# Linear attention and two expert layers: the first chunk's weights decoded over four slots of attention

## The chip, the cores and the metric

The kernel runs on one core of a Trainium2 chip. The metric is the time of the program on the device, in microseconds, as the median of several runs. Three runs of the kernel before gave 1057.95, 1059.56 and 1063.15 us.

## The reference, cut to what matters

```
phi(x) = [exp(p), exp(-p)],  p = x @ w_phi - max|x @ w_phi|      # per row, 2 x 128 features
kv = phi(k).T @ v;  z = sum over rows of phi(k)                   # per batch and head
attn = (phi(q) @ kv) / (phi(q) @ z + 1e-6)                        # (4, 8, 576, 64)
x = attn as 2304 tokens x 512
x = (sigmoid(x @ w_gate) * (x @ w_val)) @ w_out                   # d_ff 1536
out = leaky(x @ w_in2) @ w_out2                                   # d_ff 2048, slope 0.01
```

Attention's inputs are float32; the five weight matrices of the two layers are float64. The kernel reads those as pairs of int32 and builds from each a high and a low part in fp32r, and every product of a layer is three matmuls: high by high, high by low, low by high.

## The kernel before, in words

Attention is worked in 16 head pairs, (b, c) with b the batch and c the pair of heads; one pair is worked in one **slot** of the loop at line 516. A slot's order is written out by hand as a string of pieces in `ORDERS`, and `SLOTS` says which string each of the 17 slots takes (lines 502 to 511). Pieces of the slot's own pair n are: `tk`, `tq`, `tr` transpose k, q and the remaining 64 rows on TensorE (`ps_t`); `pk`, `pq` project them (`ps_p`) and take the maximum away on VectorE (L337, L339); ScalarE makes the features of k (`ka`, L346); `kv` multiplies them with v (L385, L386); `qr`, `qf` transpose the projected q (`ps_r`, `ps_q`, L397, L403) and ScalarE takes their exps (L406). Of the pair before, o, the slot computes numerator and denominator (`nn`, `ps_n`, L435), and sends the denominators on a round trip: `nm1` moves them to 9 per partition (`d`, L444), `nm2` takes reciprocals on VectorE (L449), writes them to DRAM (`rd`, L451), reads them back spread over the partitions (`rb`, L454), and GpSimd multiplies (L457). Of the pair before that, oo, `nm3` splits the normalised output into a high part on ScalarE (`xh`, L48) and a low part on VectorE (`xl`, L49).

Two streams are laid into the slots. A piece `d` takes a step of `first_weights`, which fetches the raw words of chunk 0's three matrices (512 KB each half, L116) and decodes them in six halves, each by six instructions on VectorE (L96, L99, L101, L103, L105, L108) and two on ScalarE (L97, L106); it has 22 steps. A piece `M` takes a unit of `moe_units`: three matmuls of chunk 0's gated products (`pg`, `pv`, 128x512) for batch b, or of the product with w_out (`po`). A unit of kk needs the normalised output of pair kk of its batch, and is left out while that isn't there (`ready`). 78 units exist; what the slots don't take is worked behind the loop, and then chunk 0 of the last batch, the other chunks and the second layer follow.

The strings are not the order in which instructions stand in the engines' queues. The program is recorded in the strings' order, and a scheduler then orders each engine's queue by what it expects to be ready; it pulls units of the gated product ahead as fillers. Each engine works its queue in that order. What the strings, the barrier at line 518 and buffers allow is what the change can move. In the names below, xh_78 and xl_79 are the halves for pairs 0 and 1 of batch 0, xh_80 and xl_81 those for pairs 2 and 3.

Of the kernel before, what the change touches and what calls it, by code (L numbers as in the profile page):

```python
# [19 lines left out]
def linear_attention_moe(ctx, tc, q, k, v, w_phi, w_gate, w_val, w_out, w_in2, w_out2, out):  # L20
# [5 lines left out]
    KD = DM // 128  # L26
# [210 lines left out]
    ld = att.enter_context(tc.tile_pool(name="ld", bufs=2))  # L237
# [41 lines left out]
    def load_pair(b, c):  # L279
        for nm, src in (("k", k), ("q", q)):  # L280
            t = ld.tile([128, J, 2, D], F32, tag=nm, name=nm)
            for h in range(2):
                nc.sync.dma_start(out=t[:, :, h], in_=src[b, 2 * c + h, 0:MAIN, :].rearrange("(p j) d -> p j d", j=J))
            nat[nm, b, c] = t
            if (nm, b, c) == ("k", 0, 0):
                for h in range(2):
                    nc.sync.dma_start(out=wbd[64 * h:64 * h + 64, h * NF:(h + 1) * NF], in_=w_phi)
        if c % 2 == 0:
            for nm, src in (("k", k), ("q", q)):
                t = ld.tile([128, 2, D], F32, tag=nm + "r", name=nm + "r", bufs=1)  # L290
                for h in range(2):
                    nc.sync.dma_start(
                        out=t[64 * h:64 * h + 64],
                        in_=src[b, 2 * c:2 * c + 4, MAIN:S, :].rearrange("(i h) s d -> h s i d", h=2)[h],
                    )
                nat[nm + "r", b, c // 2] = t
        vf = nat["v", b, c] = vfs[c % 2]
        for h in range(2):
            vs = v[b, 2 * c + h]
            nc.sync.dma_start(out=vf[:, 0:J, 65 * h:65 * h + 64], in_=vs[0:MAIN].rearrange("(p j) d -> p j d", j=J))  # L300
            nc.sync.dma_start(out=vf[64 * h:64 * h + 64, J, 66 * h:66 * h + 64], in_=vs[MAIN:S])
# [121 lines left out]
    def num(p, h):  # L423
        uh = wk.tile([128, S], F32, tag=f"u{h}", name=f"u{h}", bufs=2)
        for n in range(2):
            if n:
                yield
            cs = slice(288 * n, 288 * n + 288)
            ps2 = ps_a.tile([128, 288], F32, tag=f"kv{n}", name="ps_n")
            for s in range(2):  # L430
                i = 2 * h + s
                w = [z[:, s, 65 * h:65 * h + 128] for z in p.kvz]
                x = [f[:, cs] for f in p.qf[i]]
                if len(w) == 1:
                    nc.tensor.matmul(ps2, w[0], x[0], start=s == 0, stop=s == 1)  # L435
                else:
                    mm3(ps2, *w, *x, s == 0, s == 1)
            nc.scalar.copy(uh[:, cs], ps2)
        p.u.append(uh)

    def norm1(p):
        p.d = wk.tile([128, 9], F32, tag="d", name="d", bufs=2)
        for h in range(2):
            nc.sync.dma_start(out=p.d[64 * h:64 * h + 64], in_=p.u[h][64 - h:65 - h, :])  # L444

    def norm2(p):
        r = wk.tile([128, 9], F32, tag="r", name="r", bufs=2)
        nc.vector.tensor_scalar_add(p.d, p.d, 1e-6)
        nc.vector.reciprocal(r, p.d)  # L449
        rd = dr.tile([2, S], F32, tag="rd", name="rd", bufs=4)  # L450
        nc.sync.dma_start(out=rd.rearrange("h (p e) -> (h p) e", e=9), in_=r)  # L451
        p.rb = wk.tile([128, S], F32, tag="rb", name="rb", bufs=3)
        for h in range(2):
            nc.sync.dma_start(out=p.rb[64 * h:64 * h + 64], in_=rd[h:h + 1, :].to_broadcast([64, S]))  # L454
        for h in range(2):
            sl = slice(64 * h, 64 * h + 64)
            nc.gpsimd.tensor_tensor(out=p.rb[sl], in0=p.u[h][sl], in1=p.rb[sl], op=ALU.mult)  # L457

    def norm3(p):
        b, c = p.b, p.c  # L460
        split(p.rb[:, 0:MAIN], xpart(xh, b, c), xpart(xl, b, c))
        rs = slice(REM * b, REM * b + REM)
        split(p.rb[:, MAIN:S], xh[B][:, c, rs], xl[B][:, c, rs])

    def new_pair(b, c):
        p = Pair()
        p.b, p.c = b, c
        p.kf, p.tq, p.qf, p.u = [], [], [], []
        return p
# [11 lines left out]
    def moe():  # L481
        if m_next[0] is None or ready[0] < m_next[0]:
            return
        m_next[0] = next(m_gen, None)

    def moe_units():
        for b in range(B - 1):
            h = {}
            for kk in up1(0, b, h):
                yield KD * b + kk + 1  # L490
            for _ in down1(0, b, h):
                yield 0

    def step(gen, k=1):
        for _ in range(k):
            next(gen, None)
# [4 lines left out]

    ORDERS = [
# [7 lines left out]
    ]  # L510
    SLOTS = [0, 1, 2, 1, 5, 4, 3, 6, 3, 4, 3, 4, 3, 6, 5, 6, 3]
    m_gen = moe_units()
    m_next = [10 ** 6]
    dec = first_weights()
    split(wbd, wbh, wbl)
    for i in range(NP + 1):
        oo, o, n = o, n, (new_pair(*pairs[i]) if i < NP else None)
        if i == KD:
            step(dec, 100)
            p0.close()  # L520
            pools["hp"] = mid.enter_context(tc.tile_pool(name="hp0", bufs=2))
            pools["tp"] = mid.enter_context(tc.tile_pool(name="tp0", bufs=3))
            pools["po"] = ps_m
            m_next[0] = next(m_gen)
        ln = iter(())
        for piece in ORDERS[SLOTS[i]].split():
            if piece == "M":
                moe()
            elif piece == "d":
                if 1 <= i < KD:  # L530
                    step(dec)
            elif piece == "ld":
                if i + 1 < NP:
                    load_pair(*pairs[i + 1])
            elif piece[:2] == "nn":
                if o:
                    if piece[2:] in ("0", "2"):
                        ln = num(o, int(piece[2]) // 2)
                    next(ln, None)
            elif piece == "nm1":  # L540
                if o:
                    norm1(o)
            elif piece == "nm2":
                if o:
                    norm2(o)
            elif piece == "nm3":
                if oo:
                    norm3(oo)
                    ready[0] += 1
            elif n:  # L550
                fn, *arg = {
                    "tk": (t_k,), "tq": (t_q,), "tr": (t_r,), "pk0": (p_k, 0), "pk1": (p_k, 1), "pkr": (p_kr,),
                    "pq0": (p_q, 0), "pq1": (p_q, 1), "pqr": (p_qr,), "qr": (q_r,), "qf0": (q_f, 0), "qf1": (q_f, 1),
                    "kv0": (kv_main, 0), "kv1": (kv_main, 1),
                }[piece]
                fn(n, *arg)
# [339 lines left out]
```

## Time and profile before

| | |
|---|---|
| median of three runs | 1059.56 us |
| profiled execution | 1060.74 us, its span 1059.0 us |
| granted clock of TensorE, mean | 0.998 |
| TensorE busy | 1038.1 us (98%) |
| VectorE busy | 739.7 us (70%) |
| ScalarE busy | 455.8 us (43%) |
| GpSimd busy | 50.5 us (5%) |

In the rows PE is TensorE, PEld its weight loads, DVE VectorE, ACT ScalarE, POOL GpSimd and SP the engine that issues the transfers. Matmuls overlap, so the length of one is more than the distance to the next. Behind an arrow in brackets stands the idle time ahead of an instruction and what ended it. Attention runs from the start to about 270 us; slot 1 begins with its first `ps_n` at 22.0 us, slot 2 at 37, slot 3 at 57.7, slot 4 at 71.1, slot 5 at 86.7.

### The profile page before, as it was taken

To read this page: it belongs to the slowest core of one execution; us is meant where nothing else is said; L and a number is where in the kernel's file an instruction comes from. 1 tells how busy PE (TensorE), PEld (TensorE's weight loads), DVE (VectorE), ACT (ScalarE), POOL (GpSimd) and SP (SyncE) were. 2 spreads that over 40 slices of the span, in tenths; PEclk is the share of its full clock that TensorE was granted. 3 is DMA by queue.
4 is the path that set the end of the run, shared out by engine and by line. 5 is a ranking of instruction groups with operands and counts; after the bars stand their busy time and mean duration, and the time that the engine had idled before them with its cause. 6 is when DMAs were issued, how large, how long until landed. Compare 5 with 4: busy or idle time off the path is not lost.

```text
span 1059.0 us, 14600 instructions
## 1 busy us (share of the span) xinstructions
PE 1038.1 (98%) x5506; PEld 885.6 (84%) x5506; DVE 739.7 (70%) x1309; ACT 455.8 (43%) x954; POOL 50.5 (5%) x49
## 2 busy tenths in 40 slices
PE   7999999999999999999999999999999999999998
PEld 6788988889788888888888888888888888888886
DVE  4964877766469976385383457995797887979555
ACT  4666676767445332132131134475343333433221
POOL 0112121212200000000000000000000000000000
PEclk9999999999999999999999999999999999999999
DMA  5532233232174322021020013254162542515143
GB/s 144 149 86 71 68 101 78 70 85 55 52 270 119 102 71 68 1 80 40 1 80 1 1 41 150 95 193 143 56 229 76 173 148 91 178 61 179 47 161 131
DMA packets 96006, 104.46 MB, mean 99 GB/s; under 512 B 66112, under 2 KB 66240, under 8 KB 95936
## 3 DMA queue, kind: packets, MB, share of 16 engines
q1 hardware_dynamic: 95936, 103.52, 31.4%
q8 instruction: 44, 0.72, 0.3%
q14 instruction: 26, 0.21, 0.1%
HBM read 87.10 MB, written 16.33 MB: 98 GB/s over the span
## 4 chain that ended last, share of the span: by engine, by line
PE 87%; DVE 4%; DMA 4%; SPq 2%; ACT 2%; issue 1%; POOL 1%; POOLq 0%; ACTq 0%; DVEq 0%
PE ps_u L54 13%; PE ps_u L53 13%; PE ps_u L52 13%; PE ps_p L52 11%; PE ps_p L54 11%; PE ps_p L53 11%; PE kv L385 4%; PE ps_n L435 2%; DMA rb<-rd 1%; DVE ql L420 1%; DMA raw<-in_moe_w_gate_dram 1%; PE ps_q L403 1%; PE ps_t L318 1%; PE kv L386 1%; POOL rb L457 1%
## 5 line engine op out<-in xcount | busy, mean ns | idle before, releaser
L53 PE MATMUL ps_u<-xl,w 128*128 128x512 f32 (+1 forms) x592 | 213.5, 361 | 0.2 <-DVE xl L49 0.2
L52 PE MATMUL ps_u<-xh,w 128*128 128x512 f32 (+1 forms) x592 | 213.3, 361 | 0.0
L54 PE MATMUL ps_u<-xh,w 128*128 128x512 f32 (+1 forms) x592 | 212.8, 361 | 0.1
L52 PEld LDWEIGHTS ps_u<-xh,w 128*128 128x128 f32 x592 | 111.8, 189 | 17.7 <-ACT w L106 0.3
L54 PEld LDWEIGHTS ps_u<-xh,w 128*128 128x128 f32 x592 | 111.7, 189 | 17.6 <-DVE w L108 0.5
L53 PEld LDWEIGHTS ps_u<-xl,w 128*128 128x128 f32 x592 | 111.8, 189 | 17.5 <-DVE xl L49 0.5
L48 ACT CAST gh<-q 128x512 fp32r<-128x512 f32 (+1 forms) x134 | 76.2, 576 | 91.6 <-DVE q L664 89.9
L810 DVE TENSOR_TENSOR acc<-acc,ps_p 128x512 f32<-128x512 f32 x126 | 86.3, 685 | 39.7 <-PE ps_p L54 39.0
L52 PE MATMUL ps_p<-w,gh 128*128 128x512 f32 x288 | 112.1, 390 | 0.0
L53 PE MATMUL ps_p<-w,gh 128*128 128x512 f32 x288 | 112.0, 389 | 0.0
L54 PE MATMUL ps_p<-w,gl 128*128 128x512 f32 x288 | 111.7, 389 | 0.0
L49 DVE TENSOR_TENSOR gl<-q,gh 128x512 fp32r<-128x512 f32 (+1 forms) x134 | 83.9, 632 | 32.3 <-ACT gh L48 31.6
L664 DVE SCALAR_TENSOR_TENSOR q<-q,ps_u 128x512 f32<-128x512 f32 (+1 forms) x54 | 33.8, 626 | 90.0 <-PE ps_u L54 81.8
L640 DVE TENSOR_TENSOR acc<-acc,ps_p 128x512 f32<-128x512 f32 (+1 forms) x100 | 62.3, 632 | 24.6 <-PE ps_p L54 23.7
L53 PE MATMUL ps_p<-gl,w 128*128 128x512 f32 (+1 forms) x216 | 79.0, 366 | 0.0
L675 ACT ACTIVATE q<-q 128x512 f32<-128x512 f32 x48 | 30.2, 632 | 113.3 <-DVE q L753 113.2
L54 PE MATMUL ps_p<-gh,w 128*128 128x512 f32 (+1 forms) x216 | 78.8, 365 | 0.0
L52 PE MATMUL ps_p<-gh,w 128*128 128x512 f32 (+1 forms) x216 | 78.2, 366 | 0.0
L753 DVE TENSOR_TENSOR q<-ps_u,q 128x512 f32<-128x512 f32 x80 | 54.9, 688 | 24.9 <-PE ps_u L54 19.3
L106 ACT CAST w<-m 128x512 fp32r<-128x512 f32 x68 | 41.4, 619 | 68.2 <-DVE m L105 43.0
L97 ACT ACTIVATE e<-e,ebias 128x512 int32<-128x512 int32 x68 | 48.7, 722 | 43.5 <-DVE e L96 43.0
L662 ACT ACTIVATE q<-ps_u 128x512 f32<-128x512 f32 (+1 forms) x54 | 29.5, 549 | 86.9 <-PE ps_u L54 81.8
(142 smaller groups left out, 2051.5 us busy)
## 6 DMA issues: line engine op xcount, KB each, us to landing
w<-td SPq DMA_DIRECT2D x56, 512.0 KB, 4.7
raw<-in_moe_w_out_dram SPq DMA_DIRECT2D x28, 512.0 KB, 3.7
raw<-in_moe_w_in_dram SPq DMA_DIRECT2D x16, 512.0 KB, 3.7
td<-w SPq DMA_DIRECT2D x16, 512.0 KB, 2.7
raw<-in_moe_w_gate_dram SPq DMA_DIRECT2D x12, 512.0 KB, 4.1
raw<-in_moe_w_val_dram SPq DMA_DIRECT2D x12, 512.0 KB, 4.0
rb<-rd SPq DMA_DIRECT2D x32, 144.0 KB, 3.2
k<-in_k_dram SPq DMA_DIRECT2D x32, 128.0 KB, 2.9
```

The costliest lines, as they stand in the source:

```text
L48: nc.scalar.copy(hi, src)
L49: nc.vector.tensor_tensor(out=lo, in0=src, in1=hi.bitcast(F32), op=ALU.subtract)
L52: nc.tensor.matmul(ps, lh, rh, start=first, stop=False, **kw)
L53: nc.tensor.matmul(ps, lh, rl, start=False, stop=False, **kw)
L54: nc.tensor.matmul(ps, ll, rh, start=False, stop=last, **kw)
L97: nc.scalar.activation(out=e, in_=e, func=ACTF.Relu, scale=8.0, bias=ebias)
L106: nc.scalar.copy(hi, mf)
L385: nc.tensor.matmul(ps[:, h], p.kf[j // 2][:, j % 2, h, s, :], vf[:, j, 64 * h:64 * h + 65], start=(h, j) == (0, 0), stop=False)
L640: nc.vector.tensor_tensor(out=a, in0=a, in1=po, op=ALU.add)
L664: nc.vector.scalar_tensor_tensor(out=th, in0=th, scalar=1.0, in1=ps[1], op0=ALU.add, op1=ALU.mult)
L753: nc.vector.tensor_tensor(out=o, in0=x, in1=y, op=ALU.add)
L810: nc.vector.tensor_tensor(out=a, in0=a, in1=po, op=ALU.add)
```

## The change

The strings for slots 1 and 2 have 6 pieces `d` each in place of 15. Slot 4 takes the string of slot 2, with six `d` and no `M`, in place of one with five `M`. The end of decoding and the start of the units move from slot 4 to slot 5 (`KD` is 4).

```diff
-        "nn0 d tk tq d nn1 tr pk0 d d d pk1 nm3 nn2 d nn3 d pqr pq0 nm1 d pq1 d pkr d kv0 nm2 ld qr d d kv1 d qf0 qf1 d d",
...
+        "nn0 tk tq nn1 tr pk0 d pk1 nm3 nn2 d nn3 pqr pq0 nm1 d pq1 pkr d kv0 nm2 ld qr d kv1 qf0 qf1 d",
...
-    SLOTS = [0, 1, 2, 1, 5, 4, 3, 6, 3, 4, 3, 4, 3, 6, 5, 6, 3]
+    SLOTS = [0, 1, 2, 1, 2, 4, 3, 6, 3, 4, 3, 4, 3, 6, 5, 6, 3]
...
-        if i == KD:
+        if i == KD + 1:
             step(dec, 100)
...
             elif piece == "d":
-                if 1 <= i < KD:
+                if 1 <= i <= KD:
                     step(dec)
```

VectorE, the middle of slot 2, before. L96 to L108 are decoding, L337 and L339 the projections' maximum and its subtraction (`t` for k, `tr` and `tqr` for the remaining rows).

```order
L96 TENSOR_SCALAR e<-raw 128x512
L99 TENSOR_SCALAR m<-raw 128x512
L337 TENSOR_REDUCE m<-ps_p 128x4
L108 TENSOR_TENSOR w<-m,w 128x512
L101 SCALAR_TENSOR_TENSOR m<-raw,m 128x512
L103 SCALAR_TENSOR_TENSOR e<-raw,e 128x512
L339 TENSOR_TENSOR t<-ps_p,m 128x512
L105 SCALAR_TENSOR_TENSOR m<-m,e 128x512
L337 TENSOR_REDUCE m<-ps_p 128x4
L96 TENSOR_SCALAR e<-raw 128x512
L339 TENSOR_TENSOR t<-ps_p,m 128x512
L108 TENSOR_TENSOR w<-m,w 128x512
```

The same place now:

```order
L108 TENSOR_TENSOR w<-m,w 128x512
L99 TENSOR_SCALAR m<-raw 128x512
L101 SCALAR_TENSOR_TENSOR m<-raw,m 128x512
L337 TENSOR_REDUCE m<-ps_p 128x4 x2
L339 TENSOR_TENSOR t<-ps_p,m 128x512 x2
L103 SCALAR_TENSOR_TENSOR e<-raw,e 128x512 x2
L337 TENSOR_REDUCE m<-ps_p 128x2 x2
L339 TENSOR_TENSOR tr<-ps_p,m 128x256
L339 TENSOR_TENSOR tqr<-ps_p,m 128x256
L105 SCALAR_TENSOR_TENSOR m<-m,e 128x512
L49 TENSOR_TENSOR xl_79<-rb,xh_78 128x512
```

Where eight decoding instructions stood around the maxima of k before, three stand ahead of them and three behind, and the low part of pair 0's output has moved up to here.

ScalarE in slot 4, from the casts of the transposed inputs (`xhi`, `xrhi`) to the cast of pair 2's output (`xh_80`), before:

```order
L48 CAST xhi<-ps_t 128x512
L438 COPY u_897<-ps_n 128x288
L48 CAST xhi<-ps_t 128x512
L48 CAST xrhi<-ps_t 128x128 x2
L438 COPY u_897<-ps_n 128x288
L346 ACTIVATE kar<-tr 128x2x128 x2
L438 COPY u_948<-ps_n 128x288
L346 ACTIVATE ka<-t 128x4x128 x4
L438 COPY u_948<-ps_n 128x288
L48 CAST xh_80<-rb 128x512
L48 CAST xh_94<-rb 128x64
```

The same place now, with one cast of decoding (L106) in it:

```order
L48 CAST xhi<-ps_t 128x512
L438 COPY u_855<-ps_n 128x288 x2
L106 CAST w<-m 128x512
L48 CAST xrhi<-ps_t 128x128
L438 COPY u_910<-ps_n 128x288
L48 CAST xh_80<-rb 128x512
L346 ACTIVATE ka<-t 128x4x128 x4
L48 CAST xrhi<-ps_t 128x128
L438 COPY u_910<-ps_n 128x288
L48 CAST xhi<-ps_t 128x512
L346 ACTIVATE kar<-tr 128x2x128 x2
L48 CAST xh_94<-rb 128x64
```

The cast of xh_80 stood behind the four exps of `ka` and both casts of transposed inputs; it now stands ahead of the exps and of the second cast.

TensorE in slot 4, from the projection of the remaining rows to the first product with xh_80, before:

```order
L52 MATMUL ps_p<-wbh,xrhi 128x256
L53 MATMUL ps_p<-wbl,xrhi 128x256
L54 MATMUL ps_p<-wbh,xrlo 128x256
L385 MATMUL kv<-vf_124,ka 128x65 x8
L386 MATMUL kv<-vf_124,kar 128x130
L385 MATMUL kv<-vf_124,ka 128x65 x2
L52 MATMUL pg<-xh_80,w 128x512
L385 MATMUL kv<-vf_124,ka 128x65 x4
L53 MATMUL pg<-xl_81,w 128x512
L54 MATMUL pg<-xh_80,w 128x512
```

The place of that product now:

```order
L53 MATMUL ps_p<-wbl,xhi 128x256
L54 MATMUL ps_p<-wbh,xlo 128x256
L324 MATMUL ps_t<-ident,kr 128x128
L435 MATMUL ps_n<-qf,kvzf_134 128x288 x3
L54 MATMUL pv<-xh_78,w 128x512
L324 MATMUL ps_t<-ident,qr 128x128
L52 MATMUL pg<-xh_80,w 128x512
L318 MATMUL ps_t<-ident,q 128x128 x4
L52 MATMUL ps_p<-wbh,xrhi 128x256
L53 MATMUL ps_p<-wbl,xrhi 128x256
L54 MATMUL ps_p<-wbh,xrlo 128x256
L385 MATMUL kv<-vf_124,ka 128x65 x4
```

The product with xh_80 stood within the kv products; it now stands ahead of the transposes of q, of the remaining rows' projection and of all kv products.

## Rows read from the trace of the kernel before

**Rows 1.** The page: busy time of each engine, its share of the span, and instructions.

```profile
PE 1038.1 (98%) x5506; PEld 885.6 (84%) x5506; DVE 739.7 (70%) x1309; ACT 455.8 (43%) x954; POOL 50.5 (5%) x49
```

**Rows 2.** Table by stretch: stretch, length, busy us of each engine (instructions), clock, DMA, GB/s.

```profile
22.00:36.60 14.60, 14.50 (x93) 12.71 (x93) 13.09 (x25) 9.46 (x24) 0.00 (x0) 0.88 0.58 142
36.60:57.70 21.10, 17.21 (x94) 13.04 (x94) 20.04 (x38) 14.18 (x36) 2.90 (x2) 1.00 0.48 125
57.70:71.10 13.40, 13.39 (x96) 11.95 (x95) 7.72 (x14) 8.34 (x23) 2.83 (x2) 1.00 0.26 63
71.10:86.70 15.60, 15.56 (x110) 13.69 (x109) 9.43 (x20) 9.61 (x27) 2.85 (x2) 1.00 0.37 89
86.70:284.00 197.30, 191.00 (x1337) 172.08 (x1338) 136.54 (x248) 130.51 (x359) 37.00 (x24) 1.00 0.29 72
284.00:1059.00 775.00, 770.72 (x3684) 647.98 (x3682) 544.53 (x948) 275.51 (x473) 2.84 (x2) 1.00 0.31 103
```

**Rows 3.** Chain of waits, 40 to 58 us: its shares by line.

```profile
by line: DMA raw<-in_moe_w_out_dram 23.8%; DVE m L337 17.0%; DVE w L108 14.4%; DVE e L96 7.7%; DVE m L101 6.7%; DVE t L339 6.7%; DVE e L103 6.7%; DVE m L105 6.7%; PE ps_q L403 4.9%; DVE tq L339 4.2%; DVE m L99 3.7%; issue 3.0%; PE ps_n L435
```

**Rows 4.** Waits of TensorE, 15 to 90 us: total, times, longest (us).

```profile
PE ps_n L435 <- ACT qf L406: 3.2, 2, 2.6
PE ps_q L403 <- DVE tq L339: 1.6, 1, 1.6
```

**Rows 5.** VectorE by line, 22.0 to 86.7 us: busy us, mean ns, idle time before.

```profile
L105 DVE SCALAR_TENSOR_TENSOR m<-m,e 128x512 f32<-128x512 f32 x6 | 4.1, 684 | 0.0
L99 DVE TENSOR_SCALAR m<-raw 128x512 int32<-128x512 int32 x5 | 2.1, 419 | 0.0
```

**Rows 6.** Timeline of all engines, 69 to 83 us: start, length (us), instruction.

```profile
71.70 0.57 SPq L451 DMA_DIRECT2D rd<-r  x1
74.23 1.22 SPq L454 DMA_DIRECT2D rb<-rd  x2
77.73 2.92 POOL L457 TENSOR_TENSOR rb<-u,rb 64x576 f32<-64x576 f32 x2 [11.48 <-DMA rb<-rd]
80.97 0.76 ACT L48 CAST xh<-rb 128x512 fp32r<-128x512 f32 x2
```

**Rows 7.** Timeline of TensorE, the same stretch.

```profile
70.06 0.82 PE L403 MATMUL ps_q<-ident,tq 128*128 128x128 f32 x6
70.64 0.48 PE L52 MATMUL pg<-xh,w 128*128 128x512 f32 x1
71.13 0.75 PE L435 MATMUL ps_n<-qf,kvzf 128*128 128x288 f32 x2
...
79.95 0.28 PE L52 MATMUL ps_p<-wbh,xrhi 128*128 128x256 f32 x1
80.07 0.28 PE L53 MATMUL ps_p<-wbl,xrhi 128*128 128x256 f32 x1
80.31 1.90 PE L385 MATMUL kv<-vf,ka 128*128 128x65 f32 x16
```

**Rows 8.** Timeline of all engines, 138 to 147 us (slot 7).

```profile
142.07 0.40 PE L52 MATMUL po<-gh,w 128*128 128x512 f32 x1
142.30 0.40 PE L53 MATMUL po<-gl,w 128*128 128x512 f32 x1
142.32 0.77 ACT L48 CAST xh<-rb 128x512 fp32r<-128x512 f32 x2 [2.09 <-POOL rb L457]
144.41 0.36 PE L52 MATMUL ps_p<-wbh,xhi 128*128 128x256 f32 x1 [1.24 <-DVE xl L49]
```

**Rows 9.** Line 451, the transfer rd<-r, up to 140 us: issue to landing.

```profile
DMA to landing us min/median/max: 1.4/2.1/4.4
```

**Rows 10.** Table by stretch, around two gaps of TensorE.

```profile
19.40:22.10 2.70, 0.08 (x2) 0.04 (x1) 1.11 (x4) 1.36 (x3) 0.00 (x0) 1.00 1.11 276
22.10:25.50 3.40, 3.40 (x10) 2.58 (x11) 2.82 (x6) 2.45 (x8) 0.00 (x0) 0.53 0.38 79
...
53.00:57.30 4.30, 2.65 (x18) 2.15 (x18) 4.28 (x10) 1.58 (x7) 0.00 (x0) 1.00 0.31 69
```

2 rows, old and new, of the table ORDERS are left out of this document.

## The prediction

> **What bounds the kernel now.** I read the page's busy shares first: TensorE is busy for 1038.1 of 1059.0 us, so a change can pay only where TensorE stands still, 21 us in all [rows 1]. The table by stretch, cut at the points where a slot's first product of the numerator starts on TensorE, says where that is [rows 2]. Slot 1 (22.0 to 36.6) loses 0.10 us, slot 2 (36.6 to 57.7) loses 21.10 - 17.21 = 3.89, slots 3 and 4 lose 0.01 and 0.04, the other attention slots and the end of chunk 0 together 197.30 - 191.00 = 6.30, and the 775 us behind them 4.28. The part of slots 1 to 4 is thus 4.04 us, nearly all of it in slot 2. VectorE explains it: in slot 2 it is busy for 20.04 of 21.10 us, in slots 3 and 4 for 7.72 of 13.40 and 9.43 of 15.60. The chain of waits through slot 2 agrees; by lines it is VectorE's decoding, its reductions and the transfers of raw weights, with little of TensorE [rows 3]. The waits of TensorE name what came late: slot 2's q projections for 1.6 us, and once 2.6 us for the first features (of 3.2), in the gap ahead of slot 1 [rows 4].
>
> So decoding is not spread over three slots now. The order on VectorE has 12 of its 36 instructions beside slot 1's work and 24 beside slot 2's; none are left for slot 3. After the change I count 11, 12, 7 and 6 over slots 1 to 4.
>
> **The change part by part.** Slot 2 loses 12 decoding instructions on VectorE. Of the six kinds, two take about 0.42 us like L99 and four about 0.68 like L105 [rows 5], 0.60 on the mean: 12 x 0.60 = 7.2 us, which leaves 20.0 - 7.2 = 12.8 us beside 17.2 us of TensorE. Slot 1 shows what such a slot loses: VectorE is 13.09 of 14.60 there, fuller than slot 2 will be, and TensorE loses 0.10 [rows 2]. Bounds: all 3.89 us saved, or, if the 1.6 us for q stays, 2.3. I take 3.5, nearer the upper end since slot 1 is the nearest row.
>
> Slot 3 gains 7 instructions, 4.2 us: VectorE 7.7 + 4.2 = 11.9 of 13.4, as full as slot 1. One residual cast of a decoded weight (L108) stands between the two of the transposed inputs, which puts the q part of the projection back by 0.6 us. Bounds 0 and 1.2 (the wait of 1.24 us in rows 8, where a projection came late); I take +0.4. Slot 4 gains 6 instructions, 3.6 us: 13.0 of about 16, which alone costs nothing.
>
> The gated products do not begin later in the built order, though their code does: products that are ready are pulled up as fillers. TensorE has 11 of them by the end of slot 4 before and 18 now, and 55 and 61 left behind the last slot's transposes. Each keeps TensorE for 0.23 us (start to start in rows 8) wherever it stands, so the sum is unchanged and I cost this at 0. The cover is that TensorE is full at the end of chunk 0.
>
> What costs is where one of them now stands in slot 4. Gated product kk = 2 needs the normalised output of pair 2 (xh_80), and it now stands ahead of the transposes of q in TensorE's queue; ScalarE's cast that makes xh_80 stands ahead of the four exps of ka. Before, cast and product stood behind them. Both queues now stop until POOL has done pair 2. When is that? Before, slot 3's last product of kv with the values is followed by slot 3's last transposes at 70.06; then the value loads on SP come free, rd is issued at 71.70 behind them, rb at 74.23, POOL runs from 77.73 to 80.65 and the cast starts at 80.97 [rows 6]. Limited by POOL alone, xh_80 is there at 80.65 + 0.6 = 81.25, that is 11.2 us behind the last kv product. SP's order keeps the loads ahead of rd, so I keep the 11.2. From the last kv product to slot 4's start TensorE now has eight transposes (six start in 0.58 us, rows 7, so 0.8) and four gated products (0.9), so xh_80 comes 11.2 - 1.7 = 9.5 us into slot 4. TensorE gets to the product sooner: the work from 71.13 to 80.31 [rows 7] is 9.2 us, and of it the q projection (12 products, 0.12 from start to start), the remainder's (6), four transposes (0.4) and two gated products (0.46) are not ahead of it any more, three gated products (0.7) are: 9.2 - 1.4 - 0.7 - 0.4 - 0.5 + 0.7 = 6.9 us. TensorE waits for 9.5 - 6.9 = 2.6 us. Behind it stand the transposes of q and the kv products, behind the cast the ka exps (2.2 us) and the cast of q; the two sets of 16 kv products, 1.9 us each in rows 7, cover most of those. The nearest row is in slot 7 of the kernel before, where the same cast came before the exps: ScalarE stood for 2.09 us and TensorE for 1.24 [rows 8]. Bounds: rd took 2.1 us to land on the median, 1.4 at least and 4.4 at most [rows 9], so 2.6 - 0.7 = 1.9 and 2.6 + 2.3 = 4.9. I take 2.5.
>
> A gap of 2.7 us ahead of slot 1 was followed by 3.4 us at a granted clock of 0.53, the lower of the two levels (1.2 of 2.4 GHz), while the 1.65 us that TensorE lost between 53.0 and 57.3 changed nothing: 1.00 there and behind it [rows 2, 10]. The Trainium skill (TensorE: Matmul & The Clock Gate, Part 1) says that idling puts TensorE back to 1.2 GHz until it has been active again; both rows can be read that way, and by it the change may pay for its new gap twice. That rule is the second rival's. The gap stands between the two cases; in the sum I leave the clock at 1.00.
>
> The other slots keep their number of gated products in the code, but the built order puts 6 in place of 15 into slot 6 and moves others. They lose 6.30 us now; I take 0, and 2 either way as the bound: 9 fillers of 0.23 us are 2.1.
>
> Sum: -3.5 + 0.4 + 2.5 = -0.6 us. The profiled execution took 1060.74 us, so 1060.1; it lies 1.2 above the median of the three runs, 1059.56, by which it is 1059.0. I say 1059.2.
>
> **The rivals.** First, the gain is kept: pair 2's chain comes in time, because slot 2 runs faster and its loads are out sooner, and slot 4 does not wait. For it: SP's order has one load fewer between rd and rb. Against it: the 11.2 us hang on slot 3's own end, not on slot 2. Then -3.5, up to -3.9 with slot 3 free of cost: 1059.56 - 3.6 = 1056.0.
>
> Second, slower: pair 2's hold in slot 4 is 4.9 us, for which rd at its slowest is enough, and the clock falls behind it. At 0.53 for 3.4 us the loss is 3.4 x 0.47 = 1.6. Sum -3.5 + 0.4 + 4.9 + 1.6 = +3.4, so 1063.0. It decides from a hold of 3.1 us, where the gain is gone. For it: the two queues that stop, and the row of the low clock. Against it: slot 7's 1.24.
>
> Third, the change moves no decoding that matters: the q path of slot 2, not decoding, sets its length, and slot 2 saves only 2.3 us while slot 4 holds for 2.5 and slot 3 costs 0.4: +0.6, 1060.2. The full VectorE of slot 2 speaks against it.
>
> **How the numbers follow.** The forecast has 0.50, with 1057.0 to 1061.5 of its own from the bounds of the hold and the later slots; the first rival 0.24, the second 0.20, the third 0.06. Low: the first rival with 1 us from the later slots, 1055.0. High: the second with 0.8 from the later slots, 1063.8. About 0.5%, 5.3 us, is what a measurement of this kernel can tell from no change. Faster than 1054.3 needs the first rival and 2 us from the later slots: 0.05 and 0.01 for the rest. Slower than 1064.9 needs the second near its upper bound, 0.07, and 0.02 for the rest. That leaves 0.85 for no difference.
>
> **What would show it.** Right: slot 2 about 17.5 us long with under 0.8 us of TensorE's idle time; a wait of 1.5 to 4 us at a gated product pg for ScalarE's cast of xh in slot 4, and ScalarE idle there for POOL; slot 3 with under 1 us. The first rival shows no wait of TensorE over 1 us between 36 and 86 us. The second shows a granted clock near 0.5 behind slot 4's gap. I am wrong altogether if the time moves by over 5 us, which these four slots cannot give or take: then the later slots or the weights' decoding behind attention have moved.

## The result, and the profile after

The changed kernel takes 1069.80 us (median of 7 runs, 1064.89 to 1072.68) and the kernel before 1059.52 beside it: ratio 1.0089, 95% interval 1.0066 to 1.0112. Forecast were 1059.2, between 1055.0 and 1063.8, with 0.09 for slower: the forecast was wrong. The profiled execution took 1069.80 us, its span 1068.0, which is 9.0 more than before.

First the page's busy times after, which answer to [rows 1], then the table by stretch, cut as in [rows 2] where each slot's numerator starts (columns as there); the last cut is where slot 15's transposes end.

```profile
PE 1043.7 (98%) x5506; PEld 889.4 (83%) x5506; DVE 740.6 (69%) x1309; ACT 456.1 (43%) x954; POOL 51.9 (5%) x49
```

```profile
22.00:36.80 14.80, 14.50 (x93) 12.84 (x93) 12.52 (x25) 8.99 (x23) 0.00 (x0) 0.88 0.58 145
36.80:53.10 16.30, 16.11 (x97) 13.42 (x97) 14.20 (x28) 11.61 (x31) 3.46 (x2) 1.00 0.56 151
53.10:66.90 13.80, 13.79 (x98) 12.26 (x98) 11.62 (x22) 9.93 (x26) 3.18 (x2) 1.00 0.36 82
66.90:89.50 22.60, 19.84 (x111) 17.23 (x111) 12.08 (x24) 10.38 (x29) 2.80 (x2) 0.85 0.26 63
89.50:274.60 185.10, 177.15 (x1253) 158.28 (x1254) 128.22 (x235) 122.20 (x334) 34.29 (x22) 1.00 0.29 73
274.60:1068.00 793.40, 786.44 (x3763) 661.03 (x3761) 553.64 (x961) 284.72 (x498) 6.08 (x4) 1.00 0.30 101
```

TensorE is busy for 5.6 us longer with the same 5506 matmuls and idle for 3.4 longer. Busy time that grows at an equal count can come from the clock, and the rows show one new stretch for it: slot 4 is 7.0 us longer than in [rows 2], at a mean clock of 0.85. Slot 2 is 4.8 us shorter and slot 3 0.4 longer. The last two rows answer to these two of the kernel before, cut at the same points of its program:

```profile
86.70:267.90 181.20, 176.39 (x1265) 160.36 (x1265) 127.21 (x235) 122.18 (x335) 33.76 (x22) 1.00 0.30 76
267.90:1059.00 791.10, 785.33 (x3757) 659.70 (x3755) 553.86 (x961) 283.83 (x497) 6.08 (x4) 1.00 0.30 102
```

Slots 5 to 15 grow by 3.9 us with 12 fewer gated products in them (2.8 us at 0.23 each), and what is behind them by 2.3 with 6 more (1.4).

To take such shifted work out, I subtract from the distance between the starts of two successive matmuls the median of that distance for this kind of matmul in the kernel before where TensorE did not idle. The remainders are summed by slot, and called lost time below. Changed kernel less kernel before, in us: slot 1 -0.35, slot 2 -4.75, slot 3 -0.05, slot 4 +6.86, slots 5 to 15 +6.4, behind them +1.0, in all +9.1, beside 9.0 in the spans. The whole has to agree, since both kernels do the same matmuls; what this tells is the split, in which some tenths at a slot's border can fall to either neighbour.

In slot 4, the waits of TensorE from 15 to 90 us, against [rows 4], and the timeline of SP (SPq is its queue), POOL, ScalarE and TensorE, against [rows 6, 7]:

```profile
PE ps_n L435 <- ACT qf L406: 2.9, 3, 2.4
PE pg L52 <- ACT xh L48: 2.2, 1, 2.2
PE ps_q L403 <- DVE tq L339: 0.2, 1, 0.2
```

```profile
66.54 0.57 SPq L451 DMA_DIRECT2D rd<-r  x1
69.23 1.22 SPq L454 DMA_DIRECT2D rb<-rd  x2
72.46 2.87 POOL L457 TENSOR_TENSOR rb<-u,rb 64x576 f32<-64x576 f32 x2 [9.79 <-ACT xrhi L48]
75.36 0.62 ACT L48 CAST xh<-rb 128x512 fp32r<-128x512 f32 x1 [2.42 <-POOL rb L457]
75.89 2.19 ACT L346 ACTIVATE ka<-t 128x512 f32<-128x512 f32 x4
76.03 0.50 PE L52 MATMUL pg<-xh,w 128*128 128x512 f32 x1 [2.21 <-ACT xh L48]
```

And the table in steps of 2 us there; the clock is third from the end of a row:

```profile
75.00:77.00 2.00, 0.96 (x7) 0.94 (x8) 0.69 (x1) 1.64 (x4) 0.33 (x1) 1.00 0.15 33
77.00:79.00 2.00, 2.00 (x12) 2.00 (x11) 1.14 (x3) 2.00 (x7) 0.00 (x0) 0.56 0.29 65
79.00:81.00 2.00, 2.00 (x10) 1.90 (x10) 0.00 (x0) 0.77 (x4) 0.00 (x0) 0.50 0.34 75
81.00:83.00 2.00, 2.00 (x10) 1.90 (x10) 0.74 (x2) 0.00 (x0) 0.00 (x0) 0.50 0.00 0
83.00:85.00 2.00, 2.00 (x15) 2.00 (x14) 0.74 (x3) 0.27 (x1) 0.00 (x0) 0.74 0.00 0
85.00:87.00 2.00, 2.00 (x19) 1.95 (x18) 1.32 (x3) 0.27 (x2) 0.00 (x0) 1.00 0.18 41
```

TensorE and ScalarE both stop for pair 2's multiplication on POOL. Then TensorE, busy without a break, runs at half its clock (0.50, the lower of its two levels): by the shares missing in four rows 0.88 + 1.00 + 1.00 + 0.52 = 3.4 us. With 2.8 us of idle time in slot 4 (22.60 - 19.84) that is 6.2 of its 6.9.

In slots 6 to 8 TensorE's timeline has idle times that the kernel before has only in part (one of 1.24, [rows 8]); each waits for a result of VectorE that came late, with no product to fill the time:

```profile
112.12 0.39 PE L52 MATMUL ps_p<-wbh,xrhi 128*128 128x256 f32 x1 [0.75 <-DVE xrlo L49]
113.73 0.35 PE L52 MATMUL ps_p<-wbh,xhi 128*128 128x256 f32 x1 [0.28 <-DVE t L339]
125.89 0.40 PE L53 MATMUL ps_n<-ql,kvzr 128*128 128x288 f32 x1 [1.06 <-DVE ql L420]
149.60 0.35 PE L52 MATMUL ps_p<-wbh,xhi 128*128 128x256 f32 x1 [1.49 <-DVE xl L49]
```

### The profile page after: what moved, and what is told of

The parts are those of the page before. It is cut to its first block, busy times and chain, and to the rows that moved or that the text cites. A ratio compares the mean times of both kernels' runs of the same rounds, so it can differ in the third digit from the quotient of the medians.

```text
span 1068.0 us, 14601 instructions
## 1 busy us (share of the span) xinstructions
PE 1043.7 (98%) x5506; PEld 889.4 (83%) x5506; DVE 740.6 (69%) x1309; ACT 456.1 (43%) x954; POOL 51.9 (5%) x49
## 4 chain that ended last, share of the span: by engine, by line
PE 85%; DVE 4%; ACT 4%; DMA 3%; SPq 2%; POOL 1%; issue 1%; POOLq 0%; ACTq 0%; DVEq 0%
PE ps_u L53 13%; PE ps_u L54 13%; PE ps_u L52 13%; PE ps_p L52 11%; PE ps_p L54 11%; PE ps_p L53 11%; PE kv L385 5%; PE ps_n L435 2%; DVE ql L420 1%; POOL rb L457 1%; DMA rb<-rd 1%; DMA raw<-in_moe_w_gate_dram 1%; ACT qh L406 1%; PE ps_q L403 1%; PE kv L386 1%
## 5 line engine op out<-in xcount | busy, mean ns | idle before, releaser
L52 PEld LDWEIGHTS ps_u<-xh,w 128*128 128x128 f32 x592 | 111.8, 189 | 19.6 <-ACT xh L48 1.4
L106 ACT CAST w<-m 128x512 fp32r<-128x512 f32 x68 | 41.6, 622 | 62.2 <-DVE m L105 37.1
```

The costliest lines, as they stand in the source:

```text
L52: nc.tensor.matmul(ps, lh, rh, start=first, stop=False, **kw)
L106: nc.scalar.copy(hi, mf)
```

## The experiments

The eight kernels ran in two groups of four. The kernel before took 1060.22 us (17 runs) beside the first group and 1060.27 (16 runs) beside the second; ratios are against it. The changed kernel ran in neither group: differences from it are between its median and theirs, and would be some 0.7 us larger if each were taken from the kernel before beside it.

**Pair 2's parts behind slot 4's features.** The cast and what follows from it are tied to the last exp, so that the order that is built cannot put them ahead of the features:

```
+            last_exp[0] = nc.scalar.activation(out=a[:, :, :, s, :], in_=t, func=ACTF.Exp, scale=sc)
...
-                if oo:
+                if oo and i == KD:
+                    with tc.issue_after(last_exp[0].ins):
+                        norm3(oo)
+                    ready[0] += 1
+                elif oo:
```

> The changed kernel with one thing more: the normalized parts of pair 2 (xh from rb) are queued on ScalarE behind slot 4's features (ka), so that no feature and no matmul of slot 4 stands behind the transfer of rb. Theory A (slot 4's hold is followed by the half clock, together 6.9 us of TensorE's time in the profile of the changed kernel): the idle of 2.2 us and the 7.2 us at 0.50 to 0.56 both go, 5 to 7 us are won, about 1063.5. Rival B (the half clock belongs to the slot's mix of matmuls, not to the idle ahead of it): the idle goes, the clock still falls to 0.5 after 77 us, 1067.5. Rival C (the hold only comes back a slot later, at the next group that reads xh of pair 2): 1069 to 1070, with an idle of 2 us in slot 5.

1062.56 us (1059.04 to 1065.19), ratio 1.0015 [1.0005, 1.0026]: 7.2 us less than the changed kernel. ScalarE's timeline in slot 4, and the table from 75 to 90 us of the changed kernel and then of this one:

```profile
74.00 2.19 ACT L346 ACTIVATE ka<-t 128x512 f32<-128x512 f32 x4
...
77.34 0.62 ACT L48 CAST xh<-rb 128x512 fp32r<-128x512 f32 x1
```

```profile
75.00:90.00 15.00, 13.41 (x75) 12.07 (x76) 6.04 (x14) 6.35 (x18) 0.33 (x1) 0.77 0.20 43
```

```profile
75.00:90.00 15.00, 13.65 (x94) 11.47 (x94) 9.23 (x19) 9.01 (x26) 3.50 (x3) 1.00 0.42 98
```

The features come 1.9 us earlier, the half clock is gone (the mean clocks of its twelve runs are 0.997 to 1.000, those of the changed kernel's seven 0.992 to 0.998), and lost time in slot 4 is 1.5 us where it was 7.2. Theory A holds; the 1.0 us of idle time in slot 5 (for a copy of u) is no return of the hold (C). The edit moves gated products too: in the trace, from slot 6's first numerator to slot 7's, 14 of them stand, where the changed kernel has 6 and the kernel before 18.

**Two more gated products in slot 5.**

```
+        "tk M tq nn0 ... tr ld pq1 M M M M M M pqr pkr ...",   # string 7: string 4 with two more M
-    SLOTS = [0, 1, 2, 1, 2, 4, ...
+    SLOTS = [0, 1, 2, 1, 2, 7, ...
```

> The changed kernel with two more gated products in slot 5's list (6 in place of 4). Slot 4 is as in the changed kernel; from slot 7 or 8 on each slot holds as many gated products as in the kernel before or nearly so (slot 6 holds 10 groups, where the changed kernel has 6 and the kernel before 15). Theory A (slots 6 to 16 lose 6 to 7 us in the changed kernel because fewer gated products lie beside the waits of slots 6 to 8 and a count of 2 in slots 14 and 16): 3 to 5 us are won, about 1066, and the idle in slots 6 to 9 falls. Rival B (the loss of the later slots follows from the late start of slot 5 alone, by what the transfers do then): no change, 1069 to 1070.

1068.41 us (1066.27 to 1075.63), ratio 1.0082 [1.0058, 1.0106]: 1.4 less than the changed kernel, which the two intervals do not tell from nothing, and in neither theory's range. The profiled execution (1075.63 us, 7.2 above the median) shows the same trap in another place. In slot 8 the parts of pair 6 stand ahead of the features. They did so in the kernel before ([rows 8] belong, by the numerators, to slot 8), but there their cast started 8.9 us into the slot, and here 11.8; rows of ScalarE, TensorE and the table:

```profile
152.25 0.76 ACT L48 CAST xh<-rb 128x512 fp32r<-128x512 f32 x2 [3.63 <-POOL rb L457]
```

```profile
154.21 0.36 PE L52 MATMUL ps_p<-wbh,xrhi 128*128 128x256 f32 x1 [3.30 <-ACT ka L346]
```

```profile
150.00:165.00 15.00, 11.70 (x66) 10.89 (x65) 6.23 (x15) 5.66 (x15) 2.14 (x2) 0.77 0.15 39
```

**Both edits.** With both, the gated products stand in the order from slot 6 on as in the kernel before, slot for slot.

> Both edits together: the parts of pair 2 behind slot 4's features, and two more gated products in slot 5. From slot 7 on every slot holds exactly as many gated products as in the kernel before. If the two losses are separate and all there is (theory A): slot 2's gain of 4 to 5 us is what is left, 1055 to 1058, ahead of the kernel before. If slots 3 to 6 take back what slot 2 gave (rival): 1059 to 1061, as the kernel before. If the two edits overlap (one cause, not two): no more than the better of the two alone, 1063 or more.

1055.78 us (1053.03 to 1057.64), ratio 0.9954 [0.9940, 0.9968]: faster than the kernel before by 4.4 us, and 6.8 less than with the first edit alone. Waits of TensorE from 100 to 300 us, with the first edit alone and then with both (total, times, longest):

```profile
PE ps_n L53 <- DVE ql L422: 5.1, 5, 1.2
PE ps_p L52 <- DVE xl L49: 2.3, 2, 1.3
PE ps_u L52 <- ACT xh L48: 0.9, 1, 0.9
PE ps_p L52 <- DVE tr L339: 0.6, 1, 0.6
```

```profile
PE ps_n L53 <- DVE ql L422: 1.8, 3, 1.2
PE ps_p L52 <- DVE xl L49: 1.2, 1, 1.2
PE ps_p L54 <- DVE xlo L49: 1.1, 1, 1.1
```

Lost time from slot 6 on is 18.8 us in the one and 11.7 in the other, though the one has only 4 products fewer in slot 6 (14 and 18). TensorE's first two idle times of 1 us or more there, with the first edit alone, are in slots 6 and 7:

```profile
106.61 0.36 PE L52 MATMUL ps_p<-wbh,xhi 128*128 128x256 f32 x1 [1.00 <-DVE xl L49]
118.41 0.40 PE L53 MATMUL ps_n<-ql,kvzr 128*128 128x288 f32 x1 [1.19 <-DVE ql L422]
```

With both edits neither place has one. The time is theory A's: without the two losses most of slot 2's gain is left. Shown is that the 6.8 us come with the order from slot 6 on; which of its products matter is not shown.

**Late products alone:** decoding and strings 1 and 2 of the kernel before, products from slot 5 on.

```
-    SLOTS = [0, 1, 2, 1, 5, 4, ...          # against the kernel before
+    SLOTS = [0, 1, 2, 1, 2, 4, ...
-        if i == KD:
+        if i == KD + 1:
```

> The other half of the change alone: decoding of the first chunk's weights over three slots as in the kernel before, gated products from slot 5 on as in the changed kernel (slot 4 with slot 2's list). Slot 2 is as in the kernel before, so its gain of 4.7 us is not had; in the order of slot 4 the features stand ahead of the parts of pair 2. Theory A (late start costs by the later slots' counts alone): slower than the kernel before by 4 to 7 us, 1064 to 1067, with no idle of over 1 us and no half clock in slot 4. Rival B (the late start is free; all the loss came from the decoding spread into slot 4): 1059 to 1060. Rival C (slot 4's hold belongs to the late start): half clock in slot 4 here too, 1070 or more.

1065.60 us (1062.45 to 1067.70), ratio 1.0045 [1.0031, 1.0060]. No idle time over 1 us in slot 4, mean clocks of 0.998 to 1.000 in all six runs: theory A. So late products alone cost 5.4 us, with no hold in slot 4.

**Spreading alone.**

```
+        "tq M tk d tr nn0 M nn1 d pkr ... f1 d",            # string 7: string 5 of before with six d
-    SLOTS = [0, 1, 2, 1, 2, 4, ...          # against the changed kernel
+    SLOTS = [0, 1, 2, 1, 7, 4, ...
+        if i == KD:
+            m_next[0] = next(m_gen)
...
-            m_next[0] = next(m_gen)         # was under i == KD + 1
```

> The other half of the change alone: decoding spread over four slots as in the changed kernel, but slot 4 has its old list with the gated products (and six steps of decoding in it), so products begin in slot 4 as before. In the order, slot 4 still has pair 2's parts ahead of the features. Theory A (the hold comes with the spreading, which leaves slot 3 shorter and slot 4 earlier against pair 2's transfers): idle of 2 us or more and half clock in slot 4, slot 2's gain of 4.7 us, 1066 to 1069. Rival B (the hold comes with the late products): no idle of over 1 us in slot 4, 1056 to 1060.

1066.97 us (1063.31 to 1071.03), ratio 1.0060 [1.0039, 1.0081]. The time was A's, the mechanism not: in slot 4 TensorE idled for 1.08 us at a clock of 1.00, and the half clock came in slot 8, as with two more products. In the trace both kernels have the same number of gated products in every slot from 2 to 14, 12 in slot 6, though they were written to start in different slots. TensorE's idle rows, and the stretch of slot 8:

```profile
76.26 0.50 PE L52 MATMUL pg<-xh,w 128*128 128x512 f32 x1 [1.08 <-ACT xh L48]
...
94.98 0.50 PE L52 MATMUL pg<-xh,w 128*128 128x512 f32 x1 [1.76 <-ACT xh L48]
...
148.41 0.36 PE L52 MATMUL ps_p<-wbh,xrhi 128*128 128x256 f32 x1 [3.06 <-DVE tr L339]
```

```profile
150.00:165.00 15.00, 15.00 (x86) 13.52 (x85) 7.69 (x14) 8.44 (x26) 3.27 (x2) 0.79 0.28 76
```

**Two more products, and slot 8's parts behind its features** (the first edit's tie, at i == 8 in place of KD).

> The kernel with two more gated products in slot 5, and besides pair 6's parts in slot 8 queued behind the first features of that slot (as was done for pair 2 in slot 4, which is left as in the changed kernel). Theory A (two more products won only 1.4 us because slot 8 got a hold of its own, 3.3 us of idle in its profile and a clock of 0.77 over 150 to 165 us): slot 8's idle and half clock go, 1063 to 1066. Rival B (the two products are worth 1 to 2 us, whatever slot 8 does): 1067 to 1069.

1066.20 us (1062.39 to 1070.03), ratio 1.0052 [1.0034, 1.0070], 0.2 above A's range. Slot 8's lost time falls from 7.2 to 1.2 us in the two profiles, the medians differ by only 2.2, which the intervals do not tell apart: the first profile is of an execution far above its median. Of the 6.8 us that the two products are worth beside the first edit, 3.6 are found so, at the edge of what the intervals tell apart. In both profiles slot 4 lost 9.5 to 9.9 us, 2.5 more than in the changed kernel; the half clock lasted longer there, with a mean clock of 0.56 and 0.57 from 75 to 90 us, where it was 0.77. That is hardly the rest: both profiles are of the longest execution, and the median of the mean clocks is 0.995 in all three kernels. The two edits do not simply add, since the order from slot 6 on is that of the kernel before only with both; the rest stays open.

**Idle time filled.**

```
+    if piece == "tr" and i == KD:
+        with tc.issue_after(last_tr[0].ins):
+            po = ps_m.tile([128, 512], F32, tag="po", name="fill")
+            for _ in range(28):
+                nc.tensor.matmul(po[:, 0:128], ident, ident, start=True, stop=True)
```

> The changed kernel with 28 more matmuls in slot 4 (ident by ident, 128x128, into a PSUM bank that nobody reads), queued on TensorE behind the transpose of qr, where it idles for 2.2 us. In the changed kernel four transposes of this size take 0.60 us, so 28 of them keep TensorE busy for some 3 to 4 us; ScalarE's order is unchanged, so the features still stand behind pair 2's parts, and the slot's own work waits as before or longer. The order around moves a little: pair 2's first gated product goes behind the features' matmuls. Theory A (the half clock follows from the idle time): the granted clock stays at 1.00 from 75 to 90 us, slot 4 is 2 to 4 us shorter although its own work starts later, and the whole takes 1064 to 1067. Rival B (the half clock follows from what slot 4 computes): 0.5 to 0.6 for 7 us here too, 1070 to 1073.

1067.78 us (1066.44 to 1069.42), ratio 1.0067 [1.0051, 1.0083]. The 28 matmuls (two records each) took 6.4 us, nearly double the estimate, so the time lies 0.8 above A's range. It is 2.0 us below the changed kernel's, which the two intervals do not tell apart. TensorE's row, and the table:

```profile
71.78 6.42 PE L563 MATMUL fill<-ident 128*128 128x128 f32 x56
```

```profile
75.00:90.00 15.00, 14.39 (x114) 13.19 (x113) 6.57 (x16) 7.43 (x23) 2.81 (x2) 1.00 0.24 57
```

The clock stays at 1.00 while xh still stands ahead of the features on ScalarE, which waits 2.38 us for POOL. In this execution the clock stayed at 1.00 behind the idle time ahead of slot 1 too (2.37 us), so one profile proves little; but the mean clocks of the six runs are 0.996 to 1.000, and those of the changed kernel's seven 0.992 to 0.998. With the first experiment, in which slot 4 does the same work but for 3 of 9 gated products, without the idle time and without the half clock, this speaks for the idle time of TensorE (A) and against what slot 4 computes (B).

**Every later pair's parts behind the features,** on top of both edits:

> The kernel with both edits, and the same queueing behind the features for every later pair's parts too. If each slot's features ahead of the parts are a gain as in slot 4: 1051 to 1055. If the later slots had slack there, or the parts now come late for the gated products: 1055 to 1059. Nothing in a profile speaks for a half clock here.

1056.04 us (1053.35 to 1059.52), ratio 0.9956 [0.9939, 0.9973]: no more than both edits alone. Whether the later slots had slack, or lost by parts that came late for the products what they gained, this run does not tell.

## Why the prediction was wrong

- **"The other slots ... I take 0, and 2 either way": the step that failed.** It measured +7.4 us in lost time, and 6.8 between the kernels with one edit and with both. I priced a filler by its own 0.23 us; that the order of the fillers can uncover waits many times as long was left out. In slots 6 to 8 late results of VectorE showed as idle time, and with the order of the kernel before two kinds of these waits fell from 5.1 to 1.8 us and from 2.3 to 1.2. The number in slot 6, on which the working was built, does not explain the size: the trace has 18 there before and 6 after (the prediction counted 15 and 6), but with 14, under the first edit alone, the slots from 6 on lose 18.8 us, nearly as much as the 19.6 of the changed kernel. Which places in the order cost how much stays open.
- **"In the sum I leave the clock at 1.00": wrong too.** The second rival had the mechanism, but took 3.4 us at 0.53, worth 1.6, from the gap ahead of slot 1; it was 3.4 us lost. It also wanted a hold of 4.9 us: 2.2 was enough.
- **Slot 4's hold** was right in mechanism and size: 2.21 us at the product named, where 2.5 were taken. TensorE came to it 6.9 us into the slot (at 76.03 - 2.21 = 73.82, from 66.89), as worked out. Hold and clock together are what the first experiment gave back: 5.7 us of slot 4's lost time in the profiles, 7.2 us between the medians.
- **Slot 2, -3.5:** -4.75, and 16.3 us long. The bound of 3.89 was idle time alone; by lost time slot 2 had about 5.7 us to give, so waits too short to show as idle went with it.
- **Slot 3, +0.4:** 0.4 longer in the table, -0.05 in lost time. **Moved products at 0:** right for their own time.
- **"Wrong altogether if the time moves by over 5 us ...: then the later slots ... have moved":** so it was.

In sum: -4.75 + 6.86 + 7.4 - 0.4 (slots 1 and 3) = +9.1, beside 9.0 in the spans and 10.3 in the medians.

## What to carry to other kernels

Price a filler by the waits that it may cover, not by its own length, and where a change shifts the order of fillers, do not take the later slots at nothing: here orders with 12 and with 4 fewer in slot 6 cost nearly the same, and only the old order took the cost away. When an in-order queue gets an operation that waits for another engine ahead of work that others need, cost the hold and, behind an idle time of TensorE like the 2.2 us here, a stretch at half clock as a case of its own. A change that loses can still hold a gain: tying one cast behind the features and giving two fillers back made this one 4.4 us faster than the kernel before.

## What was not expected

The half clock is a matter of the execution too. In all ten profiles TensorE idles for 2.2 to 2.9 us ahead of slot 1, and in seven of them the half clock follows. The gap ahead of slot 1 ([rows 10]) was followed by 0.53 in the profile of before; in that of both edits a gap of 2.79 us at the same place was followed by 1.00. TensorE's row and the stretch behind it:

```profile
22.57 1.21 PE L437 MATMUL ps_n<-qf,kvzf 128*128 128x288 f32 x4 [2.79 <-ACT qf L408]
```

```profile
22.40:25.80 3.40, 3.23 (x19) 2.72 (x20) 3.40 (x7) 3.40 (x11) 0.00 (x0) 1.00 0.24 53
```

Slot 4's gap in the changed kernel, 2.21 us, was shorter and followed by a longer stretch. With spreading alone, an idle time of only 1.22 us at 282.4 us was followed by 3.5 us at a mean clock of 0.51; so the length of one idle time does not settle it in these traces. The rule of the Trainium skill that the prediction cites (TensorE: Matmul & The Clock Gate, Part 1: idling puts TensorE back to 1.2 GHz) agrees with the profile of the changed kernel, where 2.21 us of idle time come ahead of 0.50; the row above is an idle time of that size that the low clock did not follow. Nor did activity end the low clock soon: with two more products TensorE was busy for all of the 13.7 us from 76.7 to 90.4, at a granted clock of 0.50. Over its seven runs the changed kernel's mean clock goes from 0.992 (1072.68 us) to 0.997 and 0.998 (1064.89 and 1067.29 us); even those two are 5 to 8 us above the kernel before, so the clock is not all of the loss.
